# Top-k attention with a mixture of depths on one core: mixture, ranks and loads at other steps of the batch

## The chip, the cores and the metric

The kernel runs on one core of a Trainium2 chip. Its engines are TensorE (PE, with weight loads as PEld), VectorE (DVE), ScalarE (ACT), GpSimd (POOL) and SyncE (SP, here only a DMA queue). The metric is the device time of one execution in microseconds, the median of several runs.

## The reference

```python
scores = scale * np.matmul(q, k.transpose(0, 1, 3, 2))       # (8, 8, 576, 576)
kth = np.partition(scores, -top_k, axis=-1)[..., -top_k:-top_k + 1]   # top_k = 32
scores = np.where(scores >= kth, scores, -1000000000.0)
attn = softmax(scores)                                      # written out in the original
x = np.matmul(attn, v)                                      # bridged to (8, 576, 512)
...
for b in range(B):                                          # mixture of depths, capacity 128
    s = x[b] @ w_gate
    top_idx = np.argpartition(-s, capacity)[:capacity]
    xe = x[b, top_idx]
    ye = np.maximum(xe @ w1, 0.0) @ w2                      # 512 -> 1024 -> 512
    out[b, top_idx] = xe + 1.0 / (1.0 + np.exp(-s[top_idx]))[:, None] * ye
```

All inputs are fp32: eight batches, eight heads, 576 positions, head width 64.

## The kernel before

**Units and steps.** The attention is cut into 160 units (b, t, hp): batch, block of 128 query rows (t = 0 to 3, and t = 4 with the last 64 rows), pair of heads. A batch has 20 units (`per_batch`). A unit of t = 0 to 3 has two tiles of 128x576 scores, one for each head; a unit of t = 4 has one tile, as both heads' 64 rows share the 128 partitions (`heads_of`). These "64-row units" are the units 16 to 19 of each batch.

The loop `for n in range(-1, len(units) + 6)` (L715) is a software pipeline written out by hand. In step n it works on six units at once, in this order:

- PE turns unit n-4 (`turn_last`, `turn`: transposes of its scores `sc`, plus a matmul with `less`, which pushes scores under the bound out of reach); ACT takes the exponential into `last` and `pT`.
- `flush()` (L752) runs what stands in the list `late`: ACT's copies of side work of the step before out of PSUM.
- PE multiplies q and k of unit n+1 into `ps`; `mask` makes `less` of unit n-3 (the first tile on ACT, a second tile on POOL); ACT copies unit n+1 to `sc` (`keep`).
- PE multiplies weights and values of unit n-4 into `av` (`values`).
- DVE finds the 24th largest score of unit n (`find_bound`: `cand`, `best`) and the 32nd of unit n-2 (`find_kth`: `next8`, from `y`).
- ACT takes signs of unit n-1 against its bound (`cut`, `part`: `seen`, `sides`), POOL multiplies them with the scores (`y`) and adds a tail (`fill`).
- Once per t: DVE inverts the sums (`invert`), a step later POOL scales the block (`normalise`, x<-xs,rden) and DVE takes its gates (`gates`, `dot`); after t = 4 SP stores x of the batch to `out`.

**Side work.** Two generators take one piece each per step, behind the work above. `mixture` (L504) is the mixture of depths of the batch before: four gate transposes; one more; five pieces with a rank each on DVE (junk<-gate_row,gate counts the larger gates, `pick` compares the rank with the slots); five small matmuls that place the row numbers (`place_ps`); the row numbers `row_i` and the gather of the 128 chosen rows `xe` out of `out` (an indirect DMA on POOL, L584); two empty pieces; the transposes of `xe` and its gate; three pieces of h = relu(xe w1), with 12, 12 and 8 matmul calls; four pieces of y = h w2 with two matmuls each; the scatter, an accumulating indirect DMA on POOL (L649). `load_kq` (L186) loads k and q of the next batch: a piece that issues the first DMAs on SP, a piece with transposes of the last 64 rows (here called tails), and eight pieces with four transposes each ("row loads"), each of which also issues the fetch three ahead. `load_v` is issued at step 6 (`v_at`).

**What sets the order.** Most engine calls go through `InOrder` (L42, the line that nearly all instructions carry in the profile), which keeps the program's order on an engine; the two indirect DMAs don't, and a scheduler places them and some POOL work near them. The side work shares one PSUM bank (`ps_misc`, one buffer). The scores of two stages share `ps`, also one buffer. Two tables set the steps:

```python
load_at = (7, 10, 11, 12, 13, 14, 16, 17, 18)   # L689; the first DMAs one step before
mix_at = 8                                       # L697
```

So, in steps of a batch: gate transposes at 8 and 9, ranks at 10 to 14, placing at 15, row numbers and gather at 16, `xe` at 19, h at 0 to 2 of the next batch, y at 3 to 6, scatter at 7. From step 160 on (the drain) the mixture takes two pieces per step.

Of the kernel before, what the change touches and what calls it, by code (L numbers as in the profile page):

```python
# [10 lines left out]
ALU = mybir.AluOpType  # L11
FP32 = mybir.dt.float32
# [33 lines left out]
def kernel(  # L46
# [123 lines left out]
    late = []  # L170
# [333 lines left out]
    def mixture(row0, gate, rank, exact=False):  # L504
# [23 lines left out]

        pick = modpool.tile([P, NT, CAP], BF16, name="pick")
        for t in range(NT):  # L530
            yield
            n = R if t == J else P
            junk = modpool.tile([P, S], FP32, name="junk", tag="scratch")
            dve.tensor_scalar(
                out=junk[0:n, :],
                in0=gate_row[0:n, :],
                scalar1=gate[0:n, t : t + 1],
                scalar2=None,
                op0=ALU.is_gt,
                op1=ALU.add,  # L540
                accum_out=rank[0:n, t : t + 1],
            )
            if exact:
                break_ties(t, gate, gate_row, rank)
            dve.tensor_scalar(
                out=pick[0:n, t, :],
                in0=slot[0:n, :],
                scalar1=rank[0:n, t : t + 1],
                scalar2=None,
                op0=ALU.is_equal,  # L550
            )
# [3 lines left out]
        for t in range(NT):  # L555
# [5 lines left out]
                start=(t == 0),  # L561
                stop=(t == J),
            )
        picked = modpool.tile([P, 2], FP32, name="picked")
        late.append(lambda ps=ps: act.copy(out=picked, in_=ps[:, 0:2]))

        yield

        row = modpool.tile([P, 1], FP32, name="row")
        dve.scalar_tensor_tensor(  # L570
            out=row,
            in0=picked[:, 0:1],
            scalar=row0 if isinstance(row0, float) else row0[:, 0:1],
            in1=picked[:, 1:2],
            op0=ALU.add,
            op1=ALU.add,
        )
        row_i = modpool.tile([P, 1], I32, name="row_i", bufs=2)
        done = B if exact else int(row0) // S + 1

        dve.tensor_scalar_min(out=row_i, in0=row, scalar1=float(done * S - 1))

        xe = modpool.tile([P, HD], FP32, name="xe", tag="gy")
        nc.gpsimd.indirect_dma_start(  # L584
# [3 lines left out]
            in_offset=bass.IndirectOffsetOnAxis(ap=row_i, axis=0),  # L588
        )

        yield
        yield
        yield
        xeT = modpool.tile([P, NDC, CAP], FP32, name="xeT")
# [91 lines left out]
    per_batch = NT * NHP  # L686


    load_at = (7, 10, 11, 12, 13, 14, 16, 17, 18)  # L689
    load_steps = {}  # L690
    for b in range(B - 1):
        at = [b * per_batch + i for i in load_at]
        load_steps[at[0] - 1] = b + 1, True
        load_steps.update({n: (b + 1, False) for n in at})
    v_at = 6

    mix_at = 8  # L697
    first_tile, tiles = [], 0
    for b, t, hp in units:
        first_tile.append(tiles)  # L700
# [269 lines left out]
```

## Time and profile before

| | |
|---|---|
| median of 3 runs | 1047.77 us (1046.32 to 1048.54) |
| the profiled execution | 1048.25 us |
| its span, first to last instruction | 1046.2 us |
| busy: PE, PEld | 961.1 us (92%), 761.8 us (73%) |
| busy: DVE, ACT, POOL | 867.1 (83%), 807.5 (77%), 702.6 us (67%) |
| mean granted clock of TensorE | 0.964 |

The profiled execution lies 0.5 us above the median. All engines are busy most of the time, so the shares alone don't tell which one holds up which step. Cuts of the time at the first score matmul of each unit (ps<-kT,qT on PE) do: interval i of a batch runs from the score matmuls of step i-1 to those of step i, and so holds the values and side work of step i-1 and the turns of step i. A window row gives its length and what each engine was busy in it.

### The profile page before, as it was taken

To read this page: it belongs to the slowest core of one execution; us is meant where nothing else is said; L and a number is where in the kernel's file an instruction comes from. 1 tells how busy PE (TensorE), PEld (TensorE's weight loads), DVE (VectorE), ACT (ScalarE), POOL (GpSimd) and SP (SyncE) were. 2 spreads that over 40 slices of the span, in tenths; PEclk is the share of its full clock that TensorE was granted. 3 is DMA by queue.
4 is the path that set the end of the run, shared out by engine and by line. 5 is a ranking of instruction groups with operands and counts; after the bars stand their busy time and mean duration, and the time that the engine had idled before them with its cause. 6 is when DMAs were issued, how large, how long until landed. Compare 5 with 4: busy or idle time off the path is not lost.

```text
span 1046.2 us, 24796 instructions
## 1 busy us (share of the span) xinstructions
PE 961.1 (92%) x7922; PEld 761.8 (73%) x7922; DVE 867.1 (83%) x4966; ACT 807.5 (77%) x1953; POOL 702.6 (67%) x818
## 2 busy tenths in 40 slices
PE   4899999989999899999999899998999999998846
PEld 3588777868787777877778687876778777777724
DVE  5899899987889887998889878898879978899221
ACT  4799898967798778987799677987789867887410
POOL 3688687863788557874688737885578746888110
PEclk9699999989999999999999999999999999999978
DMA  5912022201321015111132013110151110000020
GB/s 122 250 37 47 2 76 63 52 11 42 71 47 42 12 42 106 32 32 42 30 79 47 16 42 82 36 42 11 42 107 29 28 48 7 11 2 11 2 65 13
DMA packets 123834, 49.13 MB, mean 47 GB/s; under 512 B 118960, under 2 KB 118960, under 8 KB 122672
## 3 DMA queue, kind: packets, MB, share of 16 engines
q1 hardware_dynamic: 120320, 42.88, 16.3%
q0 software_dynamic: 1792, 4.20, 2.2%
q8 instruction: 65, 1.06, 0.4%
q10 hardware_dynamic: 1584, 0.39, 0.2%
q14 instruction: 73, 0.60, 0.2%
HBM read 35.91 MB, written 11.53 MB: 45 GB/s over the span
## 4 chain that ended last, share of the span: by engine, by line
PE 53%; DVE 27%; POOL 10%; ACT 6%; issue 3%; DMA 1%; SPq 0%; POOLq 0%; ACTq 0%; DVEq 0%
PE av L42 16%; DVE cand L42 12%; PE ps L42 12%; PE ptr L42 11%; PE h_ps L42 6%; DVE next L42 6%; PE y_ps L42 5%; POOL less L42 4%; POOL y L42 4%; DVE best L42 3%; DVE junk L42 2%; DVE pick L42 2%; PE tr L42 2%; ACT sc L42 2%; POOL x L42 1%
## 5 line engine op out<-in xcount | busy, mean ns | idle before, releaser
L42 POOL TENSOR_TENSOR y<-sc,sides 128x576 f32<-128x576 f32 x288 | 367.6, 1306 | 236.8 <-ACT sides L42 173.9
L42 DVE MAX8 cand<-sc 128x8 f32<-128x72 f32 x2304 | 324.2, 218 | 69.7 <-ACT sc L42 69.4
L42 PEld LDWEIGHTS av<-v,pT 128*128 128x128 f32 (+1 forms) x2560 | 275.2, 182 | 69.5 <-issue 25.4
L42 PE MATMUL av<-v,pT 128*128 128x65 f32 (+1 forms) x2560 | 301.8, 269 | 2.8 <-ACT pT L42 2.8
L42 POOL TENSOR_SCALAR less<-sc,next 128x576 bf16<-128x576 f32 x128 | 226.0, 1765 | 31.3 <-DVE next L42 29.6
L42 DVE MAX8 next<-y 128x8 f32<-128x584 f32 x288 | 206.8, 755 | 41.4 <-POOL y L42 41.2
L42 ACT ACTIVATE sides<-sc,seen 128x576 bf16<-128x576 f32 x288 | 221.3, 769 | 7.4
L42 PE MATMUL ptr<-ident,sc 128*128 128x128 f32 x1152 | 222.9, 286 | 0.0
L42 ACT ACTIVATE pT<-ptr 128x512 f32<-128x512 f32 x288 | 169.8, 597 | 57.9 <-PE ptr L42 48.6
L42 PE MATMUL ptr<-out_of_reach,less 128*128 128x128 bf16 x1152 | 211.5, 223 | 0.0
L42 PE MATMUL ps<-kT,qT 64*128 64x288 f32 (+1 forms) x1280 | 206.3, 442 | 5.4 <-ACT qT L42 2.7
L42 PEld LDWEIGHTS <-less 128*128 128x128 bf16 (+1 forms) x1312 | 138.1, 106 | 59.8 <-POOL less L42 46.2
L42 ACT COPY sc<-ps 128x576 f32<-128x576 f32 x288 | 171.2, 646 | 11.5 <-PE ps L42 11.4
L42 PEld LDWEIGHTS ptr<-ident,sc 128*128 128x128 f32 x1152 | 165.6, 144 | 16.8
L42 DVE MAX8 best<-cand 128x8 f32<-128x64 f32 x864 | 154.2, 215 | 3.3
L42 PEld LDWEIGHTS ps<-kT,qT 64*128 64x128 f32 (+1 forms) x1280 | 107.1, 182 | 55.0 <-issue 25.5
L42 ACT ACTIVATE less<-sc,next 128x576 bf16<-128x576 f32 x160 | 124.5, 778 | 18.4 <-DVE next L42 18.4
L42 DVE MATCH_REPLACE8 cand<-best,cand 128x64 f32<-128x64 f32 x576 | 116.5, 209 | 0.0
L42 ACT ACTIVATE last<-ps 128x128 f32<-128x128 f32 (+1 forms) x160 | 43.7, 273 | 77.6 <-PE ps L42 76.8
L42 PE MATMUL ps<-out_of_reach,less 128*128 128x128 bf16 (+1 forms) x160 | 36.6, 229 | 35.7 <-POOL less L42 35.3
L42 PE MATMUL h_ps<-xeT,w 128*128 128x128 f32 x512 | 66.1, 287 | 2.4 <-ACT hT L42 1.7
L42 PEld LDWEIGHTS h_ps<-xeT,w 128*128 128x128 f32 x512 | 61.4, 198 | 4.9 <-ACT hT L42 2.4
(84 smaller groups left out, 920.6 us busy)
## 6 DMA issues: line engine op xcount, KB each, us to landing
rows<-in_k_dram SPq DMA_DIRECT2D x64, 128.0 KB, 3.0
v<-in_v_dram SPq DMA_DIRECT2D x64, 128.0 KB, 3.0
out_dram<-x SPq DMA_DIRECT2D x8, 1024.0 KB, 4.0
rows<-in_q_dram SPq DMA_DIRECT2D x62, 128.0 KB, 2.9
w<-in_moe_w_dram SPq DMA_DIRECT2D x2, 2048.0 KB, 15.8
last<-in_k_dram SPq DMA_DIRECT2D x8, 128.0 KB, 3.6
vlast<-in_v_dram SPq DMA_DIRECT2D x8, 128.0 KB, 3.4
vpair<-in_v_dram SPq DMA_DIRECT2D x16, 64.0 KB, 2.9
```

What stands on the lines that cost most here:

```text
L42: return lambda *a, **kw: self._tc.keep_in_program_order(fn(*a, **kw))
```

## The change

It moves side work to other steps and shortens the chain from ranks to gather:

- `mix_at` is 14. Gate transposes stand at steps 14 and 15. Two ranks share a piece, so the five ranks take steps 16, 17 and 18. Placing and row numbers are at 19, the gather at 0 of the next batch, `xe` at 2, h at 3 to 5, y at 6 to 9, the scatter at 10.
- The row numbers are read by DVE straight from PSUM (`tensor_reduce`, then an add and a minimum in one `tensor_scalar`), in the piece of the placing matmuls; ACT's copy `picked` is gone. The gather begins the next piece.
- Loads: tails at step 0, row loads at 1, 10 to 13 and 16 to 18, the first DMAs at step 19 of the batch before. For the first load inside the loop (batch 1, during batch 0) steps 5 to 13, first DMAs at 4.

```diff
         for t in range(NT):
-            yield
+            if t % 2 == 0:
+                yield
...
-        picked = modpool.tile([P, 2], FP32, name="picked")
-        late.append(lambda ps=ps: act.copy(out=picked, in_=ps[:, 0:2]))
-
-        yield
-
+        done = B if exact else int(row0) // S + 1
         row = modpool.tile([P, 1], FP32, name="row")
-        dve.scalar_tensor_tensor(
-            out=row,
-            in0=picked[:, 0:1],
...
+        dve.tensor_reduce(
+            out=row, in_=ps[:, 0:2], axis=mybir.AxisListType.X, op=ALU.add
         )
         row_i = modpool.tile([P, 1], I32, name="row_i", bufs=2)
-        dve.tensor_scalar_min(out=row_i, in0=row, scalar1=float(done * S - 1))
+        dve.tensor_scalar(
+            out=row_i,
+            in0=row,
+            scalar1=row0 if isinstance(row0, float) else row0[:, 0:1],
+            scalar2=float(done * S - 1),
+            op0=ALU.add,
+            op1=ALU.min,
+        )
+        yield
         xe = modpool.tile([P, HD], FP32, name="xe", tag="gy")
         nc.gpsimd.indirect_dma_start(
...
         yield
         yield
-        yield
         xeT = modpool.tile([P, NDC, CAP], FP32, name="xeT")
...
-    load_at = (7, 10, 11, 12, 13, 14, 16, 17, 18)
+    load_at = (0, 1, 10, 11, 12, 13, 16, 17, 18)
+    first_load_at = range(5, 14)
...
-        at = [b * per_batch + i for i in load_at]
+        at = [b * per_batch + i for i in (load_at if b else first_load_at)]
...
-    mix_at = 8
+    mix_at = 14
```

On DVE, before, one rank stands behind the bounds and the `next8` of each of the steps 10 to 14 (here two of them in a row, in batch 4):

```order
L42 MAX next_8674<-y 128x8 x2
L42 TENSOR_SCALAR junk,ranks<-gate_row,gate 128x576
L42 TENSOR_SCALAR pick<-slot,ranks 128x128
L42 MAX cand<-sc 128x8 x16
L42 MAX best_8746<-cand 128x8 x2
L42 MATCH_REPLACE cand<-best_8746,cand 128x64 x2
L42 MAX best_8747<-cand 128x8 x2
L42 MATCH_REPLACE cand<-best_8747,cand 128x64 x2
L42 MAX best_8748<-cand 128x8 x2
L42 MAX next_8775<-y 128x8 x2
L42 TENSOR_SCALAR junk,ranks<-gate_row,gate 128x576
L42 TENSOR_SCALAR pick<-slot,ranks 128x128
```

After, in step 16 of the same batch:

```order
L42 MAX next_9239<-y 128x8 x2
L42 TENSOR_SCALAR sums<-xs 128x8
L42 RECIPROCAL rden<-sums 128x8
L42 TENSOR_SCALAR junk,ranks<-gate_row,gate 128x576
L42 TENSOR_SCALAR pick<-slot,ranks 128x128
L42 TENSOR_SCALAR junk,ranks<-gate_row,gate 128x576
L42 TENSOR_SCALAR pick<-slot,ranks 128x128
L42 MAX cand<-sc 128x8 x8
L42 MAX best_9315<-cand 128x8
```

Two ranks now stand in a row, and the bounds behind them are of one tile (`cand` x8 where it was x16).

On POOL, before, the gather stands in step 16 between the two `y` tiles of unit 15, ahead of a normalise (x) and a two-tile `less`:

```order
L42 TENSOR_SCALAR less<-sc,next_9185 128x576
L42 COPY seen<-next_9185 128x2
L42 TENSOR_TENSOR y<-sc,sides 128x576
L584 DMA xe<-out_dram,row_i 128x512
L42 TENSOR_TENSOR y<-sc,sides 128x576
L42 TENSOR_TENSOR y<-steps,seen 128x2x8
L42 TENSOR_TENSOR x<-xs,rden 128x512
L42 TENSOR_SCALAR less<-sc,next_9268 128x576
```

After, in steps 18 to 21:

```order
L42 TENSOR_TENSOR y<-steps,seen 128x8
L42 TENSOR_SCALAR less<-sc,next_9331 128x576
L42 COPY seen<-next_9331 128x2
L42 TENSOR_TENSOR y<-sc,sides 128x576
L42 TENSOR_TENSOR y<-steps,seen 128x8
L42 COPY seen<-next_9418 128x1
L583 DMA xe<-out_dram,row_i 128x512
L42 TENSOR_TENSOR y<-sc,sides 128x576
L42 TENSOR_TENSOR y<-steps,seen 128x8
L42 COPY seen<-next_9499 128x1
L42 TENSOR_TENSOR x<-xs,rden 128x512
L42 COPY seen<-next_9600 128x1
```

The gather is behind the last `less` of the batch and the first one-tile copy of `seen`. Ahead of the last `y` here (unit 19, step 20) the scheduler has put the normalise of step 21 and a copy of `seen`.

On PE, before, the first h matmuls of a mixture stand between the values of a 64-row unit and the turn of another:

```order
L42 MATMUL ps<-kT,qT 128x288 x4
L42 MATMUL av<-v_132,pT 64x65 x4
L42 MATMUL av<-vlast_134,last 64x65
L42 MATMUL av<-v_132,pT 64x65 x4
L42 MATMUL av<-vlast_134,last 64x65
L42 MATMUL h_ps<-xeT,w_141 128x128 x12
```

After, the values ahead of them are still of a 64-row unit (step 3 has unit 19), the turn behind them is of a two-tile unit, as are both sides of the next two pieces of h:

```order
L42 MATMUL ps<-kT,qT 128x288 x4
L42 MATMUL av<-v_132,pT 64x65 x4
L42 MATMUL av<-vlast_134,last 64x65
L42 MATMUL av<-v_132,pT 64x65 x4
L42 MATMUL av<-vlast_134,last 64x65
L42 MATMUL h_ps<-xeT,w_141 128x128 x12
```

In the turn, 64x128 became 128x128: h has moved by three steps.

## Rows read from the trace of the kernel before

**Rows 1.** Windows, half-batches: us, busy PE PEld DVE ACT POOL, clock, DMA, GB/s
```profile
66.47:99.54 33.07, 32.00 (x284) 27.15 (x284) 32.11 (x197) 31.74 (x77) 29.36 (x34) 1.00 0.15 34
99.54:120.29 20.75, 20.75 (x191) 17.16 (x189) 17.32 (x85) 18.22 (x44) 18.11 (x23) 1.00 0.06 14
120.29:170.32 50.03, 48.00 (x431) 37.97 (x429) 48.01 (x294) 46.40 (x117) 36.09 (x43) 1.00 0.28 73
170.32:236.56 66.24, 60.52 (x478) 49.10 (x479) 59.91 (x324) 51.09 (x123) 49.51 (x56) 0.90 0.11 25
298.61:357.98 59.37, 54.20 (x480) 44.65 (x479) 56.69 (x307) 50.76 (x123) 48.89 (x56) 1.00 0.12 28
479.37:541.38 62.01, 62.01 (x514) 48.51 (x512) 50.78 (x314) 49.80 (x123) 37.75 (x44) 1.00 0.26 63
541.38:574.91 33.53, 32.53 (x286) 27.30 (x285) 33.24 (x184) 32.39 (x79) 29.83 (x34) 1.00 0.15 35
574.91:602.32 27.41, 23.25 (x196) 18.02 (x194) 24.17 (x126) 18.48 (x45) 19.04 (x23) 0.94 0.07 18
909.67:963.43 53.76, 47.87 (x404) 38.30 (x402) 53.02 (x284) 43.22 (x107) 45.47 (x51) 0.97 0.02 6
```

**Rows 2.** Timeline, POOL and PE, batch 4: start us, us, engine, instruction
```profile
588.63 1.06 POOL L584 DMA_INDIRECT xe<-out_dram,row_i  x1 [1.35 <-DVE row_i L42]
592.14 1.72 POOL L42 TENSOR_SCALAR less<-sc,next 128x576 bf16<-128x576 f32 x1
593.92 0.23 PE L42 MATMUL ps<-out_of_reach,less 128*128 128x128 bf16 x1 [2.48 <-POOL less L42]
```

**Rows 3.** Windows, the interval behind the stall of batch 1
```profile
226.57:236.56 9.99, 9.99 (x49) 7.84 (x49) 5.00 (x22) 4.48 (x10) 3.29 (x5) 0.50 0.00 1
```

**Rows 4.** Groups, ranks of batch 4: count | busy us, mean ns
```profile
L42 DVE TENSOR_SCALAR_CACHE_REDUCE junk<-gate_row,gate 128x576 f32<-128x576 f32 (+1 forms) x5 | 4.0, 791 | 0.0
L42 DVE TENSOR_SCALAR pick<-slot,ranks 128x128 bf16<-128x128 bf16 (+1 forms) x5 | 3.5, 706 | 0.2
L42 DVE DVE_READ_ACCUMULATOR junk<-gate_row,gate 128x1 f32 (+1 forms) x5 | 0.4, 81 | 0.0
```

**Rows 5.** The tile xe: from issue of the gather to landing
```profile
DMA to landing us min/median/max: 3.3/3.4/4.0
```

**Rows 6.** Groups, whole span: count | busy us, mean ns | idle
```profile
L42 PE MATMUL xe_ps<-ident,xe 128*128 128x128 f32 x32 | 5.3, 292 | 4.9 <-DMA xe<-out_dram,row_i 4.9
L42 PE MATMUL y_ps<-w,hT 128*128 128x512 f32 x128 | 60.6, 600 | 0.9 <-ACT hT L42 0.9
L42 PE MATMUL h_ps<-xeT,w 128*128 128x128 f32 x512 | 66.1, 287 | 2.4 <-ACT hT L42 1.7 <-ACT xeT L42 0.7
```

**Rows 7.** Windows, single and few intervals of batches 4, 1 and 0
```profile
479.37:484.29 4.92, 4.92 (x42) 3.98 (x41) 3.73 (x24) 4.21 (x11) 0.87 (x1) 1.00 0.01 3
484.29:504.06 19.77, 19.77 (x181) 16.13 (x179) 16.48 (x112) 13.98 (x35) 8.08 (x13) 1.00 0.14 56
128.91:138.22 9.31, 8.41 (x79) 5.99 (x77) 9.31 (x62) 8.82 (x23) 5.89 (x9) 1.00 0.27 114
45.55:55.38 9.83, 9.83 (x91) 8.36 (x89) 9.26 (x57) 9.68 (x25) 8.86 (x11) 1.00 0.69 148
55.38:61.08 5.70, 5.70 (x54) 4.78 (x53) 5.70 (x40) 5.24 (x13) 5.32 (x7) 1.00 0.31 71
72.46:88.50 16.04, 16.04 (x146) 13.84 (x144) 15.65 (x100) 15.59 (x39) 13.37 (x16) 1.00 0.15 35
510.41:530.29 19.88, 19.88 (x146) 14.66 (x144) 17.08 (x101) 15.47 (x37) 15.08 (x19) 1.00 0.45 101
```

**Rows 8.** Timeline, POOL in the drain
```profile
1002.94 1.65 POOL L649 DMA_INDIRECT out_dram<-gy,row_i  x1 [24.45 <-ACT gy L42]
1004.07 1.60 POOL L42 TENSOR_TENSOR x<-xs,rden 64x512 f32<-64x512 f32 x1
```

**Rows 9.** Timeline, DVE, the fifth pick of batch 4
```profile
578.70 0.25 DVE L42 TENSOR_SCALAR pick<-slot,ranks 64x128 bf16<-64x128 bf16 x1
```

More of the change, by code (lines that the diff above doesn't have):

```diff
@@ L563, in mixture @@
             )
-        picked = modpool.tile([P, 2], FP32, name="picked")
-        late.append(lambda ps=ps: act.copy(out=picked, in_=ps[:, 0:2]))
-        yield
+        done = B if exact else int(row0) // S + 1
         row = modpool.tile([P, 1], FP32, name="row")
-        dve.scalar_tensor_tensor(
-            out=row,
-            in0=picked[:, 0:1],
[L573 to L576, printed above, removed]
+        dve.tensor_reduce(
+            out=row, in_=ps[:, 0:2], axis=mybir.AxisListType.X, op=ALU.add
         )
         row_i = modpool.tile([P, 1], I32, name="row_i", bufs=2)
-        done = B if exact else int(row0) // S + 1
-        dve.tensor_scalar_min(out=row_i, in0=row, scalar1=float(done * S - 1))
+        dve.tensor_scalar(
[7 more added lines that the diff above has]
+        yield
         xe = modpool.tile([P, HD], FP32, name="xe", tag="gy")
```

## Prediction

> **What bounds the kernel now.** I read the windows view first, because the busy shares of the whole span mix two regimes. I cut the time at the start of each unit's score matmuls, so interval i of a batch holds the values and the side work of step i-1 and the turns of step i. In the first half of batch 4 (intervals 0 to 9) TensorE is busy 62.01 of 62.01 us; the second half takes 33.53 + 27.41 = 60.94 us and TensorE is busy 55.78 of them [rows 1]. Batches 2 and 3 have 59.37 us in the second half, batches 4, 5 and 6 have 60.94, and the first halves of all five are within 0.1 us of each other. So the first half is bound by TensorE and the second loses time.
>
> Batch 0 is the yardstick: the same row loads stand in its intervals 10 to 19, but no mixture, and it takes 33.07 + 20.75 = 53.82 us [rows 1]. The loss of batch 4 is therefore 0.46 us in intervals 10 to 15 and 6.66 in 16 to 19. Where it arises is in the timeline [rows 2]: POOL stands 1.35 us at the gather for `row_i` of the same step, works through what is queued behind, ends the mask `less` at 593.86, and TensorE has idled 2.48 us for that mask. The idle time is then paid again: in batch 1 the same stall is followed by an interval of 9.99 us at a granted clock of 0.50, that is the 1.2 GHz level [rows 3], where batch 0 has 20.75 / 4 = 5.19. In batch 4 the mean clock over those four intervals is 0.94 [rows 1].
>
> Why `row_i` is late: the five ranks cost VectorE 4.0 + 3.5 us per batch (junk and pick, [rows 4]), with the reads of the accumulator (0.4) about 7.9. They stand in steps 10 to 14, where VectorE without them is busy 32.11 of 33.07 us [rows 1]. That makes 32.11 + 6.8 (all but the last rank, 1.1) = 38.9 us in a stretch of 33.07: VectorE falls 5.8 us behind. TensorE loses only 0.46 us by it there, so a backlog of up to 5.8 is carried by the pipeline; what hurts is the gather that meets it.
>
> **The change, part by part.**
>
> Ranks to steps 16 to 18. VectorE is busy 17.32 of 20.75 us there in batch 0, as bounds are of one tile [rows 1]. Adding 7.9 gives 25.2, against intervals of 20.9 after the change: 4.3 us behind, under the 5.8 that costs nothing. So the ranks cost TensorE 0; if that cover were gone, each us of backlog over it is a us of the batch. The backlog is worked off in steps 3 to 9, where VectorE has 62.01 - 50.78 = 11 us to spare per first half [rows 1].
>
> Gather one step after `row_i`. In POOL's order it now stands behind the step-19 copy of `seen`; the masks `less` of two-tile units (1.72 us each, [rows 2]) are all ahead of it, and single-tile units have none on POOL. Behind it are `y` of unit 18 (needed only after a two-tile bound) and, out of step order, normalise ahead of `y` of unit 19; both have a bound's length to spare. So 0, bounds 0 to 1.35 per batch (the wait of [rows 2]). The transfer landed in at most 4.0 us [rows 5] and TensorE now wants `xe` two steps later, some 13 us. 0.
>
> Picked copy and one DVE operation out, reduce from PSUM in: ACT loses a copy of 128x2, VectorE keeps two small operations. The reduce is a new wait of VectorE on the placing matmuls; queued behind it are the bounds of unit 0. It also frees the one bank for side work, so TensorE's tail transposes of step 0 wait for it, one interval later. With VectorE 4.3 behind and about 4.7 of interval, cost 0; its failure is the third rival.
>
> First half, per batch. Interval 0, 4.92 [rows 7], loses the four `xe` transposes (5.3 / 8 = 0.66, [rows 6]) and gains five placing matmuls of two columns each, for which no more than that 0.66 can stand; I take 0.4, so 4.7. Intervals 1 to 3, until now half-steps with h (19.77, [rows 7]), become half-steps with tails, one row load and `xe`. Half-steps without any side work take 9.31 / 2 = 4.65 in batch 1, with ACT busy 8.82 of 9.31 and TensorE 8.41 [rows 7]. The extras cost in a full step: tails 5.70 - 4.92 = 0.79, a row 16.04 / 3 - 4.92 = 0.43, `xe` 0.66, together 1.9 [rows 6, 7]. TensorE has little room and ACT, which copies them out, less: between 0 and 1.9 I take 1.4, nearer the upper end by ACT's row. Sum 4.7 + 13.95 + 1.4 = 20.0.
>
> Then h in full steps. A full step with y takes 19.88 / 3 = 6.63 [rows 7]; y is 60.6 / 128 x 4 = 1.89 of it [rows 6], so a full step bare of ACT's limits is 4.74 for TensorE. h is 66.1 / 512 = 0.129 per matmul, 24, 24 and 16 of them: 3.10, 3.10, 2.07 [rows 6]. 3 x 4.74 + 8.27 = 22.5. Three y steps follow, 19.9. First half 20.0 + 22.5 + 19.9 = 62.4 against 62.01: **+0.4** (bounds -1.0 and +2.5; the upper if ACT or the backlog paces intervals 1 to 4 in full). The move of h by itself is a loss: 22.5 + 3 x 4.65 = 36.5 against 19.77 + 3 x 4.92 = 34.5; the tails, the row and `xe` that leave full steps for half-steps pay it back.
>
> Second half, batches 2 to 6. 53.82, the row loads being where batch 0 has them (the row of step 14 is swapped for four gate transposes of the same shape), plus the rest of a y step, 0.6 (0 to 1.89), plus the last gate transpose, 0.3: 54.7. Against 59.37 twice and 60.94 three times: -4.7 and -6.2. With +0.4 each: 2 x -4.3 + 3 x -5.8 = **-26.0** (bounds -36, with none of the additions, and -14, with the upper bound of the first half and 0.3 of a wait at the gather).
>
> Batch 1: first half 50.03, VectorE busy 48.01 [rows 1]; tails and a row in half-steps instead of steps 7: +0.3. Second half 66.24, with the 9.99; after 53.8 + 0.3 and 1.0 for a backlog that starts higher: 55.1. **-10.8** (-13 to -6).
>
> Batch 7: no loads, so its second half (nine intervals, 53.76, [rows 1]) becomes 53.82 - 5.19 - 7 x 0.44 + 0.6 + 0.7 = 46.9; first half unchanged. **-6.9** (-8 to -2).
>
> Batch 0: loads in steps 5 to 13 instead of 7 to 18, the same work; the queue issues them at the same point, behind the weights. SP's order changes with the loads: the first fetches of a batch stand in step 19 of the one before, so the store of x (step 5) and the load of v (step 6) come behind two or three row fetches. Each row is fetched three rows ahead of its transposes, and v is read only in the next batch: 0. Batch 0 altogether: **0** (-1 to +2).
>
> Drain. Mixture 6 is six steps later, the same matmuls. Before, POOL has the scatter (1.65) and then normalise (1.60) between the last y and the last gate transposes [rows 8]. Now normalise stands ahead of the scatter and lies under the last y matmuls. Of the 3.25 I take half, because the later mixture brings its waits for `xeT` and for the bank into these steps: **-1.6** (-3.3 to +2).
>
> Sum: -26.0 - 10.8 - 6.9 - 1.6 = -45.3. The profiled execution took 1048.25 us, its span 1046.2; the median of the runs is 1047.77. 1047.8 - 45.3 = 1002.5, I say 1002.
>
> **The rivals.**
>
> First, the backlog does reach TensorE: two ranks per step put 25.2 us of VectorE work into 20.9 [rows 1, 4], and the backlog of 5.8 that was carried had one-tile bounds behind it in which to catch up; now the short intervals 0 to 3 follow, with two-tile bounds. That speaks for it. Against it: `next8` of a step, for which ACT and POOL wait, stands ahead of the ranks of that step. If half of the 6.66 stays in seven batches: 1002 + 23 = 1025.
>
> Second, picks that are blocked. A pick took 0.25 us in one place [rows 9] and 0.71 on the mean [rows 4]. If each waits out a whole mask of 1.72 [rows 2], it takes 1.97: +6.3 us per batch, a backlog of 10.6, 4.8 over the limit, seven times: 1002 + 34 = 1036. Against: three such masks stand in steps 16 to 18, for five picks, and the rest of POOL's work there is shorter. The Trainium skill (SBUF — State Buffer, "SBUF: two separate sides") has VectorE and GpSimd share a port pair under an exclusive lock that the loser waits for in full; the spread of the picks agrees.
>
> Third, slower: the bank. If the backlog at the end of step 19 passes 4.7 us, TensorE's tails wait for the reduce, us for us, and an idle of this kind was followed by 4.8 us lost at 1.2 GHz (9.99 - 5.19, [rows 1, 3]). From a backlog of 7.5 on, six batches lose 2.8 + 4.8 each, which eats the gain; at 9 it is 9.1 x 6 = 55: 1057.
>
> Fourth, it doesn't do what it says: POOL still waits at the gather in front of work that TensorE needs, and the 6.66 stays in seven batches [rows 1]: 1002 + 47 = 1049.
>
> **How the numbers follow.** Forecast 0.64, first rival 0.18, second 0.07, fourth 0.05, third 0.06. All bounds of the forecast at once give 986 and 1030, which is further than they will go together; 988 to 1028 holds the forecast and the first rival and leaves out the other three, 0.18. A change under 0.2% can't be told from none in this kernel; the fourth is that case (0.05), the third is slower (0.06), the rest faster (0.89).
>
> **What would show it.** Right: second halves of 54 to 56 us, no TensorE idle time over 1 us and no half-clock stretch between 60 and 940 us; VectorE's bounds trailing most in steps 18 and 19; h steps of 7.5 to 7.9 us; intervals 1 to 3 between 4.5 and 5.7. Wrong: a wait of the tails on `row`, of the turns on `less` in steps 17 to 19, or of `xe_ps` on its transfer; first halves above 65.

## The result, and the profile after

The changed kernel takes **1007.92 us** (median of 4 runs, 1006.76 to 1009.17) where the kernel before, on the same chip, takes 1047.88 (1046.32 to 1048.54): a ratio of 0.9621 with a 95% interval of 0.9604 to 0.9638, so 40 us less. The forecast was 1002, in a range of 988 to 1028. The profiled execution took 1007.97 us with a span of 1006.2, against 1048.25 and 1046.2.

First the busy time of the whole span and TensorE's clock in 40 slices, on the page of the changed kernel:

```profile
PE 948.5 (94%) x7922; PEld 760.4 (76%) x7922; DVE 866.1 (86%) x4966; ACT 804.9 (80%) x1945; POOL 709.5 (71%) x818
PEclk9999999999999999999999999999999999999778
```

TensorE is busy 94% of the span instead of 92%, and the clock stays in the top tenth until the last three slices (the trace has no record of the clock in the first 42.5 us). The same cuts as in [rows 1] (window, its length, busy time of PE, PEld, DVE, ACT and POOL, clock, DMA, GB/s), for the second half of batch 1, the first of batch 2, both of batch 4, the second of batch 7, and the drain, counted from the last unit's score matmuls:

```profile
172.67:227.32 54.65, 53.09 (x475) 44.46 (x473) 54.02 (x289) 50.10 (x121) 48.48 (x54) 1.00 0.16 35
227.32:291.49 64.17, 62.13 (x516) 48.93 (x514) 59.58 (x367) 50.44 (x123) 40.40 (x48) 0.97 0.19 53
462.55:523.86 61.31, 60.40 (x516) 48.03 (x514) 56.89 (x354) 50.10 (x123) 40.31 (x48) 1.00 0.20 55
523.86:578.74 54.88, 54.64 (x480) 45.23 (x478) 50.13 (x266) 50.14 (x122) 47.58 (x52) 1.00 0.19 40
870.84:919.07 48.23, 47.07 (x408) 38.10 (x406) 44.23 (x242) 43.63 (x107) 44.26 (x48) 1.00 0.05 7
919.07:1006.20 87.13, 60.83 (x369) 44.96 (x367) 26.13 (x100) 19.83 (x48) 14.85 (x18) 0.80 0.11 27
```

The second half of batch 4 is 54.88 us instead of 33.53 + 27.41 = 60.94, and TensorE is busy 54.64 of it; batches 3, 5 and 6 are the same within 0.1. That of batch 1 is 54.65 instead of 66.24. The first half of batch 4 is 61.31 instead of 62.01. Two rows don't fit: the first half of batch 2 takes 64.17 at a mean clock of 0.97, and the drain 87.13 where it took 1046.20 - 963.43 = 82.77 before.

The stretches that answer to [rows 7] and to the last four intervals in [rows 1], all in batch 4: intervals 0 to 3, the three h steps, three y steps, and intervals 16 to 19:

```profile
462.55:482.37 19.82, 18.91 (x173) 14.24 (x171) 19.54 (x121) 17.91 (x47) 9.20 (x14) 1.00 0.30 94
482.37:503.97 21.60, 21.60 (x198) 19.12 (x198) 20.91 (x136) 16.52 (x40) 17.30 (x20) 1.00 0.18 42
503.97:523.86 19.89, 19.89 (x147) 14.67 (x145) 16.43 (x99) 15.66 (x38) 13.82 (x16) 1.00 0.14 30
557.64:578.74 21.10, 21.10 (x192) 17.32 (x190) 19.89 (x85) 18.41 (x45) 18.48 (x21) 1.00 0.12 27
```

The last four intervals, 27.41 us before, take 21.10 with TensorE busy all the time. What TensorE waited for between the middle of batch 2 and the end of batch 6 (us, times, longest), before and then after, tells what went:

```profile
PE ps L42 <- POOL less L42: 21.2, 24, 2.5
PE place_ps L42 <- DVE pick L42: 3.1, 5, 0.6
```

```profile
PE ps L42 <- POOL less L42: 1.2, 5, 0.2
```

The waits for masks shrink from 21.2 to 1.2 us, and those of the placing matmuls for a pick, 3.1 us, are gone.

Where the 40.0 us between the two spans come from, batch by batch (cut at the first score matmuls):

| | before | after | difference | forecast |
|---|---|---|---|---|
| batch 0 | 109.3 | 110.6 | +1.3 | 0 |
| batch 1 | 116.3 | 105.9 | -10.4 | -10.8 |
| batches 2 to 6 | 611.7 | 583.8 | -27.9 | -26.0 |
| batch 7 | 115.2 | 107.9 | -7.2 | -6.9 |
| drain | 82.8 | 87.1 | +4.4 | -1.6 |
| ahead of batch 0 | 11.0 | 10.9 | -0.1 | 0 |
| sum | | | -40.0 | -45.3 |

So the steady part came out within 2 us of the sum, and the miss is in the drain, with a small one in batch 0. But POOL's wait at the gather, by whose 1.35 us [rows 2] the prediction bounded the cost, is longer than before. The timeline of the changed kernel, batch 4:

```profile
583.56 1.06 POOL L583 DMA_INDIRECT xe<-out_dram,row_i  x1 [4.45 <-DVE row_i L42]
584.64 1.30 POOL L42 TENSOR_TENSOR y<-sc,sides 128x576 f32<-128x576 f32 x1
```

POOL stands 4.45 us for `row_i`, more than the 1.35 of [rows 2]. For all eight gathers, the view of the tile `xe` says what POOL sat idle for (us, times), after and then before:

```profile
  DVE row_i L42: 33.9, 8
```

```profile
  DVE row_i L42: 17.0, 8
```

The waiting has doubled, from 17.0 to 33.9 us, while 40 us were won. What differs is what stands behind the gather: before it was y, the normalise and a mask of a two-tile unit, now it is y of one-tile units and a normalise.

### The profile page after: what moved, and what is told of

It reads as the page before. It is cut to its first block, busy times and chain, and to the rows that moved or that the text cites. A ratio compares the mean times of both kernels' runs of the same rounds, so it can differ in the third digit from the quotient of the medians.

```text
span 1006.2 us, 24785 instructions
## 1 busy us (share of the span) xinstructions
PE 948.5 (94%) x7922; PEld 760.4 (76%) x7922; DVE 866.1 (86%) x4966; ACT 804.9 (80%) x1945; POOL 709.5 (71%) x818
## 4 chain that ended last, share of the span: by engine, by line
PE 59%; ACT 15%; DVE 14%; POOL 8%; issue 2%; DMA 1%; SPq 0%; ACTq 0%; POOLq 0%
PE av L42 19%; PE ps L42 13%; PE ptr L42 13%; PE h_ps L42 6%; DVE cand L42 6%; PE y_ps L42 5%; ACT sides L42 5%; POOL y L42 4%; ACT sc L42 4%; DVE next L42 3%; POOL less L42 3%; PE tr L42 2%; ACT pT L42 2%; DVE best L42 2%; ACT less L42 1%
## 5 line engine op out<-in xcount | busy, mean ns | idle before, releaser
L42 PE MATMUL ptr<-ident,sc 128*128 128x128 f32 x1152 | 217.8, 281 | 0.0
L42 PE MATMUL ps<-kT,qT 64*128 64x288 f32 (+1 forms) x1280 | 203.2, 437 | 10.7 <-ACT last L42 5.8
L42 PE MATMUL ptr<-out_of_reach,less 128*128 128x128 bf16 x1152 | 206.4, 220 | 0.0
L42 PEld LDWEIGHTS ptr<-ident,sc 128*128 128x128 f32 x1152 | 162.7, 141 | 15.8
L42 POOL TENSOR_TENSOR x<-xs,rden 128x512 f32<-128x512 f32 (+1 forms) x40 | 41.7, 1042 | 33.6 <-DVE rden L42 33.6
```

Of the source, the lines that this page charges most:

```text
L42: return lambda *a, **kw: self._tc.keep_in_program_order(fn(*a, **kw))
```

## Theories and experiments

For the steady part: **theory A**, the loss came from POOL standing at the gather with a mask behind it; **theory B**, it came from VectorE's backlog by where the ranks stand, and the gather only showed it. For the drain: a wait at its entry brought a half-clock stretch, against a drain that is longer by the work moved into it. Each ratio is against runs of the kernel before on the same chip at the same time; those took 1048.5 to 1050.3 us here, so ratios compare better than times, and differences under 0.3% are read from the traces.

| run | median us | ratio (95%) |
|---|---|---|
| gather_late | 1023.76 | 0.9752 (0.9734 to 0.9769) |
| gather_held | 1006.15 | 0.9584 (0.9566 to 0.9601) |
| mix_12 | 1019.43 | 0.9707 (0.9688 to 0.9725) |
| mix_12_mask_first | 1006.51 | 0.9585 (0.9554 to 0.9616) |
| mix_13 | 1007.39 | 0.9596 (0.9571 to 0.9621) |
| last_11 | 1003.67 | 0.9576 (0.9557 to 0.9594) |
| last_13 | 1003.13 | 0.9556 (0.9535 to 0.9577) |
| drain_busy | 1001.79 | 0.9539 (0.9517 to 0.9560) |
| busy_to_end | 999.73 | 0.9513 (0.9493 to 0.9532) |
| pick_fp32 | 1007.97 | 0.9599 (0.9586 to 0.9612) |
| before_pick_fp32 | 1050.67 | 1.0004 (0.9993 to 1.0015) |
| both_fixes | 1002.67 | 0.9537 (0.9519 to 0.9555) |

**gather_late: the gather alone, in the kernel before.**

```diff
         dve.tensor_scalar_min(out=row_i, in0=row, scalar1=float(done * S - 1))
+        yield
         xe = modpool.tile([P, HD], FP32, name="xe", tag="gy")
-        nc.gpsimd.indirect_dma_start(
+        pool.indirect_dma_start(
...
-        yield
         yield
         yield
         xeT = modpool.tile([P, NDC, CAP], FP32, name="xeT")
```

> The kernel before, with one thing changed: the gather of xe is issued one step later and held to the program's order on POOL, so that it stands behind step 17's mask and y instead of in front of step 16's second y; ranks, placing, row numbers, h, y and loads stay where they were. Theory A, the stall at the gather causes the loss of the second halves: POOL's 17.0 us of waiting for row_i (8 gathers) go, TensorE gets back 6.7 us in each of batches 4 to 6, about 5 in 2 and 3, about 10 in batch 1, some 40 us in all, so 1008 to 1014 us. Theory B, the loss comes from where the ranks stand (VectorE 5.8 us behind in two-tile steps), and the gather only happens to be what it shows at: the wait moves to next8 or less, and less than 10 us come back, 1038 to 1048 us.

Measured: 26.0 us less (1049.7 x 0.0248), between the two theories, so the place of the gather alone gives 26 of the 40 us. Windows of batch 4 (second half, then its last four intervals) and the view of `xe`:

```profile
531.56:588.65 57.09, 54.19 (x479) 44.65 (x478) 56.08 (x303) 50.75 (x123) 49.33 (x56) 1.00 0.12 29
565.09:588.65 23.56, 21.66 (x195) 17.34 (x193) 22.83 (x121) 18.34 (x45) 19.50 (x23) 1.00 0.09 22
  DVE row_i L42: 8.3, 1
```

The wait at the gather is gone but for the last mixture (8.3 us, once), and intervals 16 to 19 take 23.56 us, 3.85 less than before. The changed kernel has 21.10, another 2.46 less. Who holds these is in POOL's timeline of the same batch:

```profile
568.32 1.72 POOL L42 TENSOR_SCALAR less<-sc,next 128x576 bf16<-128x576 f32 x1 [1.95 <-DVE next L42]
574.36 1.72 POOL L42 TENSOR_SCALAR less<-sc,next 128x576 bf16<-128x576 f32 x1 [1.54 <-DVE next L42]
```

POOL now waits for `next8` itself, 1.95 and 1.54 us, with nothing of the gather ahead. Of the 2.46 us that are left, TensorE's waits in these four intervals are 1.9 (1.3 for masks, 0.6 for a pick); the rest is side work that stands elsewhere in the changed kernel. So both theories hold a part: of the 6.3 us of these four intervals the gather explains 3.9 and the backlog some 2. Between the middle of batch 2 and the end of batch 6 the waits for masks are 9.6 us here, against 21.2 before and 1.2 in the changed kernel.

**gather_held: the wait at the gather taken out of the changed kernel.**

```diff
-        nc.gpsimd.indirect_dma_start(
+        pool.indirect_dma_start(
             out=xe,
```

> The changed kernel, with the gather held to the program's order on POOL, behind y of units 18 and 19 instead of in front of them. In the changed kernel POOL still waits for row_i, 33.9 us in 8 gathers. Theory A, that wait is harmless there, since behind it stand only y of one-tile units and no mask: the time stays within 2 us of the changed kernel's 1007.9. Theory B, the wait delays y of units 18 and 19, then next8 and the turns of steps 2 and 3: removing it gains 1 to 2 us in each of seven batches, 994 to 1001 us.

Held to the program's order, the gather stands behind y of units 18 and 19. The wait for `row_i` in the view of `xe`, and the second half of batch 4:

```profile
  DVE row_i L42: 6.6, 1
523.98:578.86 54.88, 54.64 (x480) 45.23 (x478) 50.13 (x266) 50.16 (x122) 47.55 (x52) 1.00 0.19 40
```

27 us of POOL's waiting are gone, and the halves are 61.33 and 54.88 us, those of the changed kernel to 0.02. The wait is harmless there: theory A. (The ratio of 0.9584 is under the changed kernel's 0.9621, but pick_fp32 below, whose batches repeat the changed kernel's too, has 0.9599: the ratios of kernels with the same stages differ by this much from one set of runs to another, so it is no gain.)

**mix_12 and mix_12_mask_first: ranks in two-tile steps, and what stands behind a small wait.**

```diff
-    load_at = (0, 1, 10, 11, 12, 13, 16, 17, 18)
+    load_at = (8, 9, 10, 11, 14, 15, 16, 18, 19)
...
-    v_at = 6
+    v_at = 7
...
-    mix_at = 14
+    mix_at = 12
```

> The changed kernel with the mixture two steps earlier in every batch: gate transposes at 12 and 13, ranks at 14 to 16 (two of the three in two-tile steps), placing at 17, gather at 18, xe at 0, h at 1 to 3 and y at 4 to 7; tails at 8, row loads at 9, 10, 11, 14, 15, 16, 18 and 19. Theory A, the position of the ranks matters little as long as no mask stands behind a waiting gather, and h in half-steps saves about as much as tails and rows in full steps cost: 1000 to 1010 us, first halves 60 to 62 us. Theory B, ranks must stand in one-tile steps: VectorE is 5 to 7 us behind at step 16 and TensorE waits for masks in steps 17 to 19, 2 to 5 us in each of seven batches: 1020 to 1040 us.

Measured: 1019.43, between the two, close to theory B, and the ratio is about 1.1% over that of the changed kernel's twin, pick_fp32. The second half of batch 4 takes 57.23 us, and this interval lost most:

```profile
572.44:580.12 7.68, 6.03 (x52) 4.55 (x50) 7.33 (x30) 4.39 (x11) 5.49 (x7) 0.91 0.01 2
```

Interval 18 takes 7.68 us, of which the last 1.3 are at half clock. The timelines of POOL and then PE show the mechanism of [rows 2] at another instruction:

```profile
575.20 1.04 POOL L42 TENSOR_TENSOR x<-xs,rden 128x512 f32<-128x512 f32 x1 [1.54 <-DVE rden L42]
576.22 1.72 POOL L42 TENSOR_SCALAR less<-sc,next 128x576 bf16<-128x576 f32 x1
578.00 0.23 PE L42 MATMUL ps<-out_of_reach,less 128*128 128x128 bf16 x1 [1.22 <-POOL less L42]
```

POOL waits 1.54 us at the normalise (x<-xs,rden) for `rden`, which VectorE, late, makes behind `next8`:

```profile
573.39 1.42 DVE L42 MAX8 next<-y 128x8 f32<-128x584 f32 x2
574.92 0.20 DVE L42 RECIPROCAL rden<-sums 128x8 f32<-128x8 f32 x1
```

The mask behind it had its `next8` at 574.81, so some 1.1 us of that wait would have been the mask's own; what the order costs is the other 0.4 us and the 1.04 of the normalise itself. TensorE waits 1.22 us for that mask. So one line was moved: the normalise of a step goes behind the mask of that step.

```diff
-        if normalising is not None:
-            b, t, xs_, rden = normalising
...
         if tiles_of(n + 1):
             scs[n + 1] = keep(tiles_of(n + 1), ps)
+        if normalising is not None:
+            b, t, xs_, rden = normalising
...
```

> The run mix_12 with POOL's normalise of a step put behind the mask and the copy of seen of that step instead of in front of them. In mix_12 interval 18 of batch 4 takes 7.68 us instead of 5.30: POOL stands 1.54 us at the normalise for rden, which VectorE, 9.1 us behind, delivers late, with a mask queued behind, and TensorE waits 1.22 us for that mask. Theory A, a backlog costs when POOL stands at a small operation of the lagging VectorE in front of a mask: 2 to 3 us come back in each of batches 2 to 7, 1003 to 1009 us. Theory B, the mask is late by the backlog itself (its next8 comes late too): less than 1 us per batch comes back, 1013 us or more.

```profile
521.37:576.41 55.04, 53.79 (x480) 44.64 (x479) 51.62 (x276) 49.98 (x124) 46.86 (x51) 1.00 0.12 26
567.73 1.72 POOL L42 TENSOR_SCALAR less<-sc,next 128x576 bf16<-128x576 f32 x1 [1.36 <-DVE sums L42]
```

13 us came back (1006.51), as theory A said: POOL still waits 1.36 us for VectorE, but at the mask itself, with the normalise behind it, and TensorE's wait for that mask is 0.22 us. The second half is 55.04 us instead of 57.23, and so it is in batches 2 to 4; batches 5 to 7 gain 0.6 to 0.7 us each, and 2.8 of the 12.3 us between the two profiled executions lie in batch 0, whose clock at the start differs from execution to execution. The first half, 61.95 us, is close to that of the kernel before (62.01), whose order of h, y, tails and rows it nearly has.

**mix_13: how much backlog is free.**

```diff
-    mix_at = 14
+    mix_at = 13
...
-    load_at = (0, 1, 10, 11, 12, 13, 16, 17, 18)
+    load_at = (0, 9, 10, 11, 12, 15, 16, 17, 19)
...
```

The part left out lets a row load and the first DMAs of the next batch stand in one step.

> The changed kernel with the mixture one step earlier: ranks at 15 to 17 (one of the three in a two-tile step), placing at 18, gather at 19, xe at 1, h at 2 to 4, y at 5 to 8; tails at 0, row loads at 9, 10, 11, 12, 15, 16, 17 and 19. VectorE's backlog should peak between the 7.4 us of the changed kernel and the 9.1 us of mix_12. Theory A, the backlog is free up to a point that lies at 8 us or more: second halves of 54.9 to 55.5 us, 1004 to 1010 us. Theory B, each us over 7.4 costs: second halves of 56 us and more, 1012 to 1018 us.

VectorE's distance is read as the time from a unit's first score matmul on PE to its first `cand` on DVE. For unit 18 of batch 4, in the changed kernel and then in mix_13, with mix_13's interval 18:

```profile
568.15 1.19 PE L42 MATMUL ps<-kT,qT 64*64 64x288 f32 x8
575.59 1.17 DVE L42 MAX8 cand<-sc 128x8 f32<-128x72 f32 x8
```

```profile
566.40 1.19 PE L42 MATMUL ps<-kT,qT 64*64 64x288 f32 x8
575.44 1.16 DVE L42 MAX8 cand<-sc 128x8 f32<-128x72 f32 x8
566.40:572.15 5.75, 5.46 (x50) 4.35 (x49) 5.51 (x24) 4.37 (x11) 5.21 (x7) 1.00 0.27 62
```

7.44 us in the changed kernel, 9.04 in mix_13. There intervals 18 and 19 take 5.75 and 5.70 us instead of 5.30: TensorE waits 0.29 us for a mask in the one and 0.44 for a pick in the other, where the placing matmuls stand now. So the greater distance costs some 0.7 us per batch, in a second half of 54.40 us, which is otherwise short, as y and the row loads stand elsewhere. Its time, 1007.39, doesn't differ from the changed kernel's. It is theory A's time, with a second half even shorter than it said; in this order the distance begins to cost between 7.4 and 9.0 us, and a little over it costs little. The distance alone doesn't set the price: in mix_12 it reaches 9.1 us in batch 4 and TensorE waits 2.0 us in the second half, in mix_12_mask_first 10.0 and 1.3 us.

**last_11 and last_13: the last batch's mixture earlier.**

```diff
-        if 0 < b < B and i == mix_at:
+        if 0 < b < B and i == (11 if b == B - 1 else mix_at):   # last_13: 13
```

> The changed kernel, but in the last batch (which has no loads) the mixture of batch 6 starts at step 11 instead of 14, so its placing stands at step 156, xe at 159 and h at the first drain step, as in the kernel before. Theory A, the drain lost time because the placing matmuls of step 159 waited 1.35 us for pick and a half-clock stretch of 13.65 us followed: the wait goes into a full step, the stretch shrinks to 3.4 us or goes, and 4 to 6 us come back, 1002 to 1004 us. Theory B, the half-clock stretch comes with the drain whatever stands in it, or the drain is longer since it holds xe and h: at most 1.5 us come back, 1006.5 or more. Theory C, ranks in two-tile steps 13 to 15 of that batch cost as much as the drain gains: within 1 us of 1007.9, with the lost time between 865 and 920 us.

> The changed kernel, but in the last batch the mixture of batch 6 starts at step 13, one step earlier than in the others: ranks at 155 to 157, placing at 158, xe and the first h in the drain. Theory A, as in last_11 the placing no longer waits at the entry of the drain, so no half-clock stretch between 920 and 960 us, and with two of three rank pieces in one-tile steps the 3.1 us that last_11 lost in steps 17 and 18 of the last batch shrink to about 1: drain 82 to 83 us, 1001 to 1003 us. Theory B, any late placing is followed by the stretch: 1006 to 1009 us.

Second half of batch 7 and drain of last_11, then the drain of last_13:

```profile
867.02:918.26 51.24, 47.65 (x413) 38.40 (x411) 46.96 (x254) 43.84 (x107) 43.97 (x48) 1.00 0.05 7
918.26:999.80 81.54, 54.37 (x364) 39.30 (x362) 22.91 (x88) 19.77 (x48) 15.68 (x19) 0.88 0.11 29
```

```profile
918.11:1001.30 83.19, 55.84 (x368) 40.78 (x367) 22.89 (x94) 19.98 (x47) 14.89 (x18) 0.87 0.11 28
```

The drains take 81.54 and 83.19 us instead of 87.13, at a mean clock of 0.88 and 0.87 instead of 0.80, and there is no half-clock stretch between 920 and 955 us in either. The second halves of batch 7 take 51.24 and 50.41 us instead of 48.23, so 3.0 and 2.2 us of the gain are lost there: in last_11 TensorE waits 2.3 us for masks and 1.2 for a pick in that stretch, in last_13 1.9 us for masks. In the traces this half and the drain together take 2.6 and 1.8 us less than in the changed kernel, less than theory A's 4 to 6 for last_11; the ratios alone (0.9576 and 0.9556, with gather_held at 0.9584) wouldn't show it. Both runs move work and so don't say whether the idle time or the work set the clock.

**drain_busy: the wait filled, nothing moved.** In the changed kernel the drain begins so, on PE:

```profile
927.70 0.17 PE L42 MATMUL place_ps<-place,pick 64*128 64x2 bf16 x1 [1.35 <-DVE pick L42]
929.80 0.98 PE L42 MATMUL av<-v,pT 128*64 128x65 f32 x8 [0.69 <-ACT pT L42]
940.12 4.62 PE L42 MATMUL h_ps<-xeT,w 128*128 128x128 f32 x24 [0.68 <-ACT xeT L42]
930.00:943.65 13.65, 12.29 (x70) 10.04 (x69) 4.55 (x15) 4.46 (x11) 4.47 (x8) 0.50 0.25 97
```

The last placing matmul waits 1.35 us for `pick`, the next values 0.69 for `pT`, and from 930.00 on the clock is at half for 13.65 us, though TensorE is busy 12.29 of them; the first 24 h matmuls take 4.62 us.

```diff
+        if n == len(units) - 1:
+            for _ in range(4):
+                pe.matmul(ps[:, 0, 0, 0:P], w1[:, 0, 0:P], w1[:, 0, 0:P])
         next(mixing, None)
```

> The changed kernel with four matmuls of 128x128 added in step 159, ahead of the placing matmuls, with results that nothing reads: some 1.05 us of work where TensorE waited 1.35 us for pick. Theory A, that idle time brought the half-clock stretch of 13.65 us in the drain: the stretch goes or shrinks to 3.4 us, and 4 to 6 us come back, 1002 to 1004 us. Theory B, the stretch comes from the many idle pieces of 0.7 us in the short one-tile steps of the drain, not from this one: the drain stays at 86 to 88 us, 1007 to 1009 us.

```profile
925.50 1.05 PE L42 MATMUL ps<-w 128*128 128x128 f32 x8
927.09 0.17 PE L42 MATMUL place_ps<-place,pick 64*128 64x2 bf16 x1 [0.46 <-DVE pick L42]
929.18 0.68 PE L42 MATMUL av<-v,pT 128*64 128x65 f32 x8 [0.69 <-ACT pT L42]
935.98 2.94 PE L42 MATMUL h_ps<-xeT,w 128*128 128x128 f32 x24 [0.68 <-ACT xeT L42]
929.40:943.05 13.65, 11.58 (x113) 9.55 (x112) 4.53 (x15) 6.42 (x16) 4.45 (x8) 1.00 0.26 98
918.46:999.50 81.04, 55.51 (x377) 40.77 (x375) 26.14 (x100) 19.63 (x48) 14.85 (x18) 0.88 0.12 29
```

With 1.05 us of matmuls in that place the wait for `pick` is 0.46 us, the clock stays at full over the same stretch, the h matmuls take 2.94 us, and the drain 81.04 instead of 87.13. The program's other work there is the same, so it was the wait: theory A. All three traces with these four matmuls (this one, busy_to_end, both_fixes) have full clock in that place, and the three of the changed order without them (the changed kernel, gather_held, pick_fp32) have the stretch of 13.65 us. Of the 6.1 us, 5.2 lie ahead of the scatter of mixture 6; the other 0.9 come in the last mixture, where the half-clock stretch is 13.65 us instead of 17.07. 81.04 is also 1.7 less than the 82.77 before.

**busy_to_end: the same in the last mixture.** `keep_busy(idle, n)` is n such matmuls into an unused bank, for the last batch's mixture alone: 2 behind the first gate transposes, 14 ahead of the placing matmuls, 14 behind them.

> The run drain_busy with TensorE kept at work in the mixture of the last batch too: 2, 14 and 14 matmuls of 128x128, whose results nothing reads, behind the first gate transposes, ahead of the placing matmuls and behind them, about 0.26 us each, in places where TensorE waits 0.7, 5 and 4.7 us. In drain_busy 13.65 us of these 37 us, from 963.02 on, were at half clock. Theory A, that stretch comes from the idle time there: it goes, the transposes of xe and the first h take 0.54 and 3.1 us instead of 1.09 and 4.51, and some 2 us come back, 999 to 1001 us. Theory B, the added work runs at half clock and stands in front of the placing and of xe: no gain or a loss of up to 4 us, 1001 to 1006 us.

```profile
919.30:998.20 78.90, 61.62 (x436) 47.26 (x435) 26.12 (x100) 19.61 (x47) 14.88 (x18) 0.96 0.12 30
```

The drain takes 78.90 us, 2.1 less, at a mean clock of 0.96; the transposes of `xe` take 0.60 us and the first h 2.94. A half-clock stretch of 3.41 us is left, and the last 3.0 us. The ratios of the two runs overlap in their intervals, so the gain is read from the drains. At 999.73 us this is the fastest kernel of the study, 4.9% under the kernel before.

**pick_fp32, before_pick_fp32, both_fixes: a theory that fell.** Why was `pick` late in step 158? Two rows of DVE in the changed kernel, and two of POOL:

```profile
921.17 0.74 DVE L42 TENSOR_SCALAR pick<-slot,ranks 128x128 bf16<-128x128 bf16 x1
922.19 1.28 DVE L42 TENSOR_SCALAR pick<-slot,ranks 128x128 bf16<-128x128 bf16 x1
919.88 1.98 POOL L42 TENSOR_SCALAR less<-sc,next 128x576 bf16<-128x576 f32 x1 [0.87 <-DVE next L42]
922.13 1.28 POOL L42 TENSOR_TENSOR y<-sc,sides 128x576 f32<-128x576 f32 x1
```

A pick takes 0.25 us alone; these take 0.74 and 1.28 and end at 921.91 and 923.47, just behind the mask and the y of POOL (921.86 and 923.41). All 16 picks of over 0.35 us in the changed kernel end like this, 0.05 us behind an instruction of POOL. The Trainium skill (SBUF — State Buffer, "Who interferes with whom") says that a `tensor_scalar`, but not the form that writes its accumulator, can take the port pair that VectorE shares with GpSimd, and that the loser then waits for the whole instruction; the trace agrees, as the counting `junk`, of that form, takes 0.79 us on the mean and 0.82 at most in both kernels.

```diff
-    slot = const.tile([P, CAP], BF16, name="slot")
+    slot = const.tile([P, CAP], FP32, name="slot")
```

> The changed kernel with the constant slot, which pick reads, in fp32 instead of bf16; nothing else. In its trace 16 of 40 picks take over 0.35 us (0.25 alone), and all 16 end together with an instruction of POOL; the two of 0.74 and 1.28 us in step 158 delay the placing of step 159. Theory A, a bf16 pick waits until POOL is done and one that reads fp32 does not: all picks take about 0.25 us, the placing of step 159 no longer waits 1.35 us, the half-clock stretch of the drain goes, and the drain takes 81 to 82 us: 1002 to 1004 us. Theory B, the placing waits for VectorE's backlog of 7.4 us whatever the picks take, or fp32 picks wait as well: drain of 86 us or more, 1006 to 1009 us.

> The kernel before with the constant slot in fp32 instead of bf16; nothing else. Its 40 picks take 23.4 us together, about 10 if none waits for POOL. Theory A, the waiting picks push the row numbers behind the moment at which POOL comes to the gather: 1.7 us less of backlog per batch let the stall at the gather (1.35 us in batch 4) and the half-clock stretch behind it go, and 15 to 30 us come back, 1018 to 1033 us. Theory B, the backlog comes from the counting of gates (4.0 us per batch) and the gather stays in front of the masks: less than 10 us, 1038 to 1048 us.

> The run busy_to_end with slot in fp32 as well. Theory A, both work by the same means in the drain (placing of step 159 without a wait), so that together they give little more than busy_to_end: 997 to 1000 us. Theory B, the picks cost time in the other batches too (TensorE or VectorE's backlog): 1 us or more per batch comes back on top, below 995 us.

```profile
922.46 1.23 DVE L42 TENSOR_SCALAR pick<-slot,ranks 128x128 bf16<-128x128 f32 x1
927.96 0.17 PE L42 MATMUL place_ps<-place,pick 64*128 64x2 bf16 x1 [1.42 <-DVE pick L42]
```

Picks that read fp32 wait just as long, so these runs took away no wait: pick_fp32 takes 1007.97 us, as theory B said, before_pick_fp32 1050.67 against the 1050.0 of the kernel before, and both_fixes 1002.67, outside both of its theories, which gives nothing over busy_to_end. That the waiting picks alone make the placing late is argued from the rows; a pick that doesn't wait wasn't tried, and VectorE is also further behind there, 9.6 us at unit 158 against 7.44 at unit 18 of batch 4.

## Why the prediction was right where it was, and where it was wrong

**Batches 2 to 6: right in size, and with one reason missing.** Second halves of 54.9 us against the 54.7 of the sum, in all five. VectorE's backlog grows as forecast: from 3.2 us at unit 16 (560.82 - 557.64) to 7.44 at unit 18, 4.3 us. The step "a backlog of up to 5.8 is carried by the pipeline; what hurts is the gather that meets it" was too simple: gather_late shows that in the order of before some 2 us of the last four intervals were the backlog itself, at 9.4 us of distance (unit 14 there: 553.60 on PE, 562.99 on DVE). The 5.8 was too small as well: the distance in the kernel before grows from 2.0 us at unit 7 of batch 4 to those 9.4. The forecast didn't suffer, as the change removes both.

**The gather "0".** The cost was right; its bound of 1.35 us, taken from the wait of [rows 2], rested on a wait that didn't shrink but grew to 4.45 us. What the prediction gave as its reason, that the masks stand ahead and what is behind has time to spare, is what counts; gather_held shows it.

**First half: +0.4 forecast, -0.7 measured** (in batches 3 to 6). Intervals 0 to 3 take 19.8 us (20.0), the y steps 19.9. The h steps take 21.60 (7.31, 7.59 and 6.70) instead of 22.5 (7.84, 7.84 and 6.81): the first of them still holds the values of a one-tile unit, unit 19 (interval i has the values of step i-1), and I counted three full steps; that is 0.5 of the 0.9. So the move of h, with the tails, a row and `xe` that go the other way, is no loss: mix_12, with nearly the order of before, has 61.94.

**Batch 1 and batch 7** came within 0.4 us, by errors that cancel: in batch 7 the second half took 48.23 instead of 46.9, and the first, which I had left unchanged, became 1.7 us shorter.

**Batch 0: 0 forecast, +1.3 measured, and not from the change.** Its first three intervals differ by the granted clock: the profiled execution of the kernel before had 6.83 us at full clock from 14.8 us on, that of the changed kernel none until 42.5 (its 128x128 transposes take 0.42 us up to there, 0.27 at full clock). Executions of the changed loads that had it (last_11, last_13, drain_busy) take 108.9 to 109.0 us against 109.3 before; those that hadn't take 110.5 to 110.7 (the changed kernel, gather_held, both_fixes), against 111.0 and 111.6 for before_pick_fp32 and gather_late, which have the loads of before. Like with like, it is a gain of 0.3 to 1.1.

**Drain: -1.6 forecast, +4.4 measured; the step that failed.** I weighed the normalise ahead of the scatter, which did move: it runs at 958.37, under y, and TensorE's wait for the last gate, in the kernel before

```profile
1006.55 0.33 PE L42 MATMUL tr<-ident,gate 64*128 64x64 f32 x1 [3.19 <-DVE gate L42]
```

is 0.68 us in the changed kernel, at 966.67. That is 2.5 us for this term, which was weighed at 1.6. (That drain_busy has a drain 1.7 us shorter than before is near the forecast by chance: it also has 19.4 us at half clock there, the kernel before 24.5.) What I left out is that the last placing now stands at the entry of the drain, where one-tile steps without loads leave nothing else for TensorE to do, so that a late rank is idle time, 1.35 us here, and that the clock then fell: 13.65 us at 1.2 GHz, about 6 us with what follows (drain_busy). It took the drain past the +2 that I gave as its worst. The prediction had the mechanism in hand for the stall of batch 1 [rows 3] and priced it only for the bank.

**The rivals.** The backlog that reaches TensorE: hardly here (1.2 us of waits for masks from the middle of batch 2 to the end of batch 6), but it begins not far above, at 9.0 us (mix_13). Blocked picks: they are there, but cheap in the steady steps: five take 2.0 us in batch 4 instead of the 3.5 of [rows 4], and they show only in the drain. The bank: VectorE's reduce waited 0.3 us in all for the placing matmuls. "It doesn't do what it says": POOL does still wait at the gather, and it costs nothing.

**The signs.** Intervals 1 to 3 (4.77, 5.44 and 4.82 us) and VectorE's greatest distance, at unit 18, are as the prediction said, and the h steps are a little shorter; two signs are not: TensorE idles 1.17 us for a mask at 177.39, in batch 1, and 1.35 at 927.70, and there are half-clock stretches at 233.68 and 930.00.

**Left open.** The first half of batch 2 takes 64.17 us instead of 61.3. Its interval 0 is 1.3 us longer, with waits of 0.41 and 0.70 us on PE at 231.3 and 232.1, and its interval 1 is 1.5 us longer, with a half-clock stretch of 3.41 us at 233.68. The stretch is in the traces of gather_held and drain_busy too, and not in that of last_11; what brings it wasn't settled. No run tried the shorter chain to the row numbers or the moved loads alone, so their shares in the 40 us aren't shown.

## What to carry to other kernels

A wait on an in-order engine costs what is queued behind it, not what it lasts: ask which instruction the bottleneck needs that stands behind, and put small operations that depend on a lagging engine behind it. A backlog is free up to some distance (here 7.4 us at steps of 5.3), so read the distance between engines and what waits at its end, not the busy share of one. And look at the last step of a stage apart from the steady ones: the same wait that is covered in the loop can be bare where the loop ends, and cost several times its length in TensorE's clock.

## What the runs showed of the hardware that was not expected

An idle time of 1.35 us and one of 0.69 two us later were followed by 13.65 us at half clock, in which TensorE was busy 12.29 us; with the first of them filled but for 0.46 us, TensorE stayed at full clock in that place and got through 113 matmuls in 13.65 us instead of 70. And picks of 0.25 us (0.28 with fp32) that wait for POOL take up to 1.28 us with bf16 and 1.25 with fp32.
